# Attention beside a gated linear unit on one core: the score tiles of a period in another order, the first one whole, two of them under one exponential

## The chip, the core and the metric

The kernel runs on one core of a Trainium2 chip. The metric is the device time of one execution in microseconds (us); for the kernel before it is 1671.07 us, the median of three runs (1670.6 to 1671.36). The core's engines work side by side, each through its own list of instructions: PE multiplies matrices (PEld is its loading of weights), ACT (ScalarE) evaluates functions such as the exponential, DVE (VectorE) reduces and combines, POOL (GpSimd) does elementwise work on the on-chip memory SBUF, SP issues DMAs. Matrix products land in PSUM, which has eight banks of 128 x 512 float32 each. Before an engine writes a bank again, those who read it must be done, and they tell so by semaphores.

## The reference

For `x` of 2048 tokens by 512 (float32):

```
q, k, v = split(x @ wqkv)                # 32 heads of width 16
p = softmax(q @ k.T / 4)                 # per head, 2048 x 2048
a = concat_heads(p @ v) @ wo
b = (sigmoid(x @ w_gate) * (x @ w_up)) @ w_down      # inner width 1792
g = sigmoid(sum(x * gate_w))
out = g * a + (1 - g) * b
```

## The kernel before, in words

Most matrix products take float32 operands that are split into a high and a low part and sum three products of them. The kernel has three stretches: a head (projections of q, k, v and the first work on the scores), 256 **periods** of attention, and a tail that multiplies by `w_down` and `wo`.

A period `k` stands for 4 key tiles of 128 keys and 512 queries, for both heads of a pair. The scores of one key tile and one head are one matmul of 64 rows by 512 columns, which fills one bank (word `t0` for head 0 of the pair, `t1` for head 1, function `st_part`, lines 630 to 644); ACT turns the bank into exponentials in SBUF (line 643). To keep the exponentials in range each query needs the maximum of its scores: for it the scores are computed a second time with queries on the partitions (words `m0`, `m1`, function `sm_step`, line 299, 48 rows by 512 columns) and DVE reduces each bank to one column (line 301). These run ahead of the exponentials by a pair of heads. The products of the gated linear unit are the filler: words `d0`, `d1` (lines 153 and 173, 64 rows by 512 columns, into the eighth bank, `dn`), twelve in a period; when a run of twelve is done, ACT copies `dn` out (line 574).

A matmul of 64 or 48 rows uses one half of the PE's rows. Words that end in 0 use the lower half, words that end in 1 the upper half, and the two halves work at the same time. An even period has `t0` (both of the period's key groups of head 0), an odd one `t1`; the filler of a period goes to the other half.

At the end of a period stand the **values** (function `values`, line 781): 32 recorded matmuls over all 128 rows that multiply the exponentials of period `k` by `v` into one bank. ACT copies that bank to SBUF (line 786, tile `part` or `sum`), and POOL adds it up (line 799).

The order inside a period is written out by hand in the strings `STEADY` (one for even, one for odd periods, lines 835 and 836) and followed by `emit`; all engines but SP keep the order of the program. Seven banks are handed out in a ring by `place`: each `t`, each `m` and the values take the next bank. In the strings of before, the first score tile of a period is cut in two pieces of 192 and 320 queries (`CUT`), and each piece takes a bank of its own. So a period takes 9 `t`, 8 `m` and one bank for the values, 18 in all, and the values get the bank that the 11th tile of the same period had. `STEADY` holds for 248 periods; the last eight follow other strings (`LAST`, lines 837 and 838), with no `m` and nothing cut, and their banks come from the same ring.

Of the kernel before, what the change touches and what calls it, by code (L numbers as in the profile page):

```python
# [2 lines left out]

# [9 lines left out]
F32 = mybir.dt.float32  # L13
F32R = mybir.dt.float32r
AF = mybir.ActivationFunctionType
# [4 lines left out]
PSUM = bass.MemoryType.PSUM  # L20
DRAM = bass.MemoryType.DRAM
SHARED = "both halves of the PE write one bank"
SYNC = mybir.DependencyInfo(mybir.DependencyClass.Sync, mybir.DependencyReason.DATA)

S, D, H, DH, F = 2048, 512, 32, 16, 1792
P = 128
# [8 lines left out]
KR = 64  # L35
# [6 lines left out]
EARLY = NPER - TAIL - 4  # L42
LOW, UP = 0, 1
AHEAD = 4
CUT = (192,)
MIX = ((((0, 0), "+", (1, 1)), ((0, 0), None, None)), (((0, 1), "-", (1, 1)), ((1, 0), "-", (0, 0))),
       (((0, 0), "+", (0, 1)), ((1, 0), "+", (1, 1))), (((1, 1), None, None), ((1, 1), None, None)))
BLOCKS = (((0, 0), (1, 0)), ((1, 1), (1, 1)), ((0, 0), (1, 1)), ((1, 0), (0, 1)), ((0, 0), (0, 0)), ((0, 1), (0, 1)))
# [2 lines left out]
@with_exitstack  # L51
def gated_mix(ctx, tc, x, xc, xmix, wqk, wv, wo, w_gu, w_down, gate_w, out):
    nc = tc.nc
    pe, act, dve, pool, sp = nc.tensor, nc.scalar, nc.vector, nc.gpsimd, nc.sync

    ctx.enter_context(tc.manual_schedule(engines=ORDERED))
    keep = ctx.enter_context(tc.tile_pool(name="keep", bufs=1))
    dram = ctx.enter_context(tc.tile_pool(name="dram", bufs=1, space=DRAM))
    ps = ctx.enter_context(tc.tile_pool(name="ps", bufs=1, space=PSUM))

    def turns(tiles):
        turn = iter(range(1 << 30))
        return lambda: tiles[next(turn) % len(tiles)]
# [1 line left out]
    def ring(pool, n, shape, name):  # L65
        return turns([pool.tile(shape, F32, name=f"{name}{i}") for i in range(n)])

    banks = [ps.tile([P, 512], F32, name=f"st{i}") for i in range(3)]
    bank = turns(banks)
    dn = ps.tile([P, 512], F32, name="dn")  # L70
    bankd = turns([dn])
    maxb = [ps.tile([P, 512], F32, name=f"sm{i}") for i in range(4)]
    bankm = turns(maxb)

    q_d = dram.tile([2, D, S], F32, name="q_d")
    k_d = dram.tile([2, D, S], F32, name="k_d")
# [19 lines left out]
    def mid(name, dt=F32):  # L96
        return keep.tile([P, 4, 512], dt, name=name, tag="mid", bufs=3)
# [44 lines left out]
    class Sum:  # L142


        def __init__(self, o, ab):
            self.o, self.n, self.last, self.token = o, 0, None, None
            self.ops = list(terms(ab))
            self.left = [list(self.ops), list(self.ops)]

        def half(self, g):  # L150
# [3 lines left out]
            if self.token:  # L154
                tc.add_manual_dep(mm.ins, self.token.ins.name, SYNC, reason=SHARED)
            self.last, self.token = mm, None
# [34 lines left out]
    def turn(*runs):  # L191

        token = pool.nop()
        tc.add_manual_dep(token.ins, runs[-1].last.ins.name, SYNC, reason=SHARED)
        for r in runs:
# [179 lines left out]
    def take(n, behind=None):  # L375
        while parts and n:
            load = parts.pop(0)()
            if behind:
                tc.add_manual_dep(load.ins, behind.ins.name, SYNC, reason="one at a time")
            n -= 1  # L380
# [111 lines left out]
    def filling():  # L492
# [45 lines left out]
        for cp in range(2):  # L538
            for fp in range(NF // 2):
# [28 lines left out]
                if cp == 0 and fp == NF // 2 - 1:  # L568
# [9 lines left out]
    first = [(j, i) for j in [*range(0, 12, 2), *range(1, 8, 2), *range(12, FIRST, 2), *range(9, FIRST, 2),  # L578
                              *range(FIRST, UPPER, 2)] for i in range(2)]
# [11 lines left out]
    for c in range(NC):  # L591
# [9 lines left out]
        for w, dst in ((w_q, q_d), (w_k, k_d)):  # L601
            o = bank()
# [21 lines left out]
    for t in range(2):  # L624
        o = bankv()
# [1 line left out]
        put_v(t, o, act)  # L627
    ptile = {}

    def st_part(k, b, first=()):  # L630

        p, r = divmod(k, 16)
        c, kt = divmod(4 * r, 16)
        qs, ks = QS[p % 2], KS[p % 2]
        r = 64 * b
        pt = ptile[k, b] = mid(f"p{k}_{b}")
        for a in range(4):
            ends = [0, *(first if a == 0 else ()), 512]
            for lo, hi in zip(ends, ends[1:]):
                o = bank()[:, :hi - lo]  # L640
                pe.matmul(o, ks[r:r + KR, (kt + a) * P:(kt + a + 1) * P], qs[r:r + KR, c * 512 + lo:c * 512 + hi],  # L641
                          start=True, stop=True)
                act.activation(pt[:, a, lo:hi], o, AF.Exp, scale=DH ** -0.5)  # L643
                yield

    closed = []
    ahead = st_part(0, 1)
    bank = bankm
# [27 lines left out]

    for _, turned in closed:
        turned()()
    seven = [maxb[0], maxb[1], banks[2], maxb[2], banks[1], maxb[3], banks[0]]
    chunks = [(c, f) for c in range(NC) for f in range(0, NF, 2)]  # L680

    def hidden_load(c, f):
# [138 lines left out]
    def emit(order, **parts):  # L821

        for word in order.split():
# [7 lines left out]
            else:  # L831
                if next(parts[word], place) is place:
                    place()

    STEADY = ("t0 m1 t0 d1 t0 d1 m0 d1 t0 m0 d1 d1 t0 d1 work t0 m0 d1 t0 d1 m0 d1 t0 d1 m0 d1 t0 d1 m1 m0",
              "t1 m0 t1 d0 t1 d0 m1 d0 t1 d0 m1 t1 d0 d0 work d0 t1 m1 t1 d0 d0 d0 m1 t1 d0 m1 t1 d0 m1 m0")
    LAST = ["t0 d1 t0 d1 t0 d1 t0 d1 d1 work t1 t1 t1 t1", "t0 d1 t0 d1 t0 d1 t0 d1 work t1 t1 t1 t1"] * 2 + [
        "t0 t0 t0 t0 work t1 d0 t1 d0 t1 d0 t1 d0 d0", "t0 t0 t0 t0 work t1 d0 t1 d0 t1 d0 t1 d0"] * 2

    group = {"m0": mx(0), "m1": mx(1), "d0": dense(LOW), "d1": dense(UP)}  # L840
    for a, engine in enumerate((act, dve)):
        put_v(NS - 2 + a, two[a].o, engine)
    bank = bankm = place
    stages = [[], []]
    ahead_h = []
    for k in range(NPER):
        n = 2 * k
        if 320 <= n < 448 and n % 16 == 0:
            logit_load((n - 320) // 8)
        if n % 32 == 0 and n // 32 + 1 < NPAIR:  # L850
            pair = load_pair(n // 32 + 1)
        if n % 32 <= 10:
            list(islice(pair, 2))
        if k >= NPER - TAIL:
            group["t0"], group["t1"] = st_part(k, 0), st_part(k + 1, 1) if k + 1 < NPER else iter(())
        elif k % 2 == 0:
            group["t0"] = chain(st_part(k, 0, CUT), st_part(k + 1, 0))
        else:
            group["t1"] = chain(st_part(k, 1, CUT), st_part(k + 1, 1))
        emit(STEADY[k % 2] if k < NPER - TAIL else LAST[k - NPER], **group)  # L860
        jobs = [turned() for turned in stages.pop(0)]
        stages.append([])
        while full:
            halves, turned = close_max()
            jobs.append(halves)
            stages[1].append(turned)
        if run is None:
            pass
        elif run.done():
            run = next(fill, None)  # L870
        elif k < NPER - TAIL or k == NPER - TAIL + 3:
            turn(run)
        if EARLY <= k < EARLY + 6:
            for _ in range(2 if k < EARLY + 3 else 1):
                weights_ahead()
        if n in (304, 308, 312, 316):
            ahead_h.append(hidden_ahead((n - 304) // 4))
            next(ahead_h[-1])
        if n in (308, 312, 316, 320):
            next(ahead_h[(n - 308) // 4])  # L880
        work(3 if isinstance(run, Sum) and k % 2 else 4)
        urgent.extend(jobs)
        if 320 <= n < 448:
            t = (n - 320) // 16 * 2
            if n % 16 == 2:
                logit_terms(t, 0)
                logit_terms(t, 1)
            elif n % 16 in (8, 10):
                logit_sum(t, (n % 16 - 8) // 2)
        if EARLY <= k < EARLY + 4:  # L890
            early_exp(*divmod(k - EARLY, 2))
        if k == NPER - 1:
            break
        values(k)
        if k == EARLY - 2:
            loaded.extend(hidden_load(*chunks[m]) for m in range(2))
        if NPER - TAIL <= k < NPER - TAIL + 4:
            early_hidden(*divmod(k - NPER + TAIL, 2))
        if n == NSTEP - 16:
            raws = [late_raw(*late[m][:2]) for m in range(2)]  # L900
        if n == NSTEP - 10:
            denominators(0)
# [41 lines left out]
    bankt = turns([dn] + maxb[2:] + maxb[:2])  # L944
# [29 lines left out]
    heads = {}  # L974
    for n, (c, f) in enumerate(chunks):
        if f == 0:
            down = [bankt() if 4 * c + t != AHEAD else None for t in range(4)] if c else seven[3:]
        if n == 4:
            g = g0[:, AHEAD:AHEAD + 1]
            dve.tensor_scalar(ahead, dn, g, None, op0=ALU.mult)  # L980
        if n in at:
            heads_out(at[n], heads.pop(at[n]))
        hl = ready[n]
        for t in range(4):
            if 4 * c + t == AHEAD:
                continue
            ops = list(terms([((hl[0][a][:, t * P:(t + 1) * P], hl[1][a][:, t * P:(t + 1) * P]), wd[f + a])
                              for a in range(2)]))
            for m, (a, b) in enumerate(ops):
                pe.matmul(down[t], a, b, start=(f == 0 and m == 0), stop=(f == NF - 2 and m == 5))  # L990
            if f == NF - 2:
                finish(4 * c + t, down[t], g0)
            if n == t == 0:
                last_values()
        if n + 5 < len(chunks):
            loaded.append(hidden_load(*chunks[n + 5]))
        if n == 9:
            denominators(1)
        if n + 3 < len(chunks):
            hidden(n + 3)  # L1000
        if n + 2 < len(chunks):
            hidden_split(n + 2)
        if n + 3 in at:
            u = at[n + 3]
            heads[u] = heads_split(u, *heads[u])
        if n + 5 in at:
            u = at[n + 5]
            heads[u] = heads_load(u)
        late_next()
# [44 lines left out]
```

## Time and profile before

| | |
|---|---|
| median of three runs | 1671.07 us |
| profiled execution, its own time | 1671.01 us |
| its span (first to last instruction) | 1669.2 us |
| granted PE clock | 1.00 |
| first values of the 256 periods | at 90.17 us of the span |
| values of the 248th period | at 1444.57 us |
| busy between 84.6 and 1444.6 us (1360.0) | PE 1359.15, DVE 1237.68, ACT 1206.48, POOL 977.93 |

The busy time of PE counts any matmul in flight, and the ends of matmuls are modelled, so it does not tell whether both halves of the rows were in use. The profile's rows of the timeline read: start in us, duration in us, engine, line, operation, written tile, read tiles, shapes, how many; brackets give the idle time before and what ended it.

### The profile page before, as it was taken

The page shows a single profiled execution, that of the slowest core. Times are in us where ns is not written, and L with a number is a line of the kernel's source. Part 1 is how long each engine was busy: PE and PEld are TensorE (multiplying, and loading weights), DVE is VectorE, ACT ScalarE, POOL GpSimd, SP SyncE. Part 2 cuts the span into 40 slices and gives each one's busy share as a digit, 9 for nine tenths or more (in the row PEclk, how much of TensorE's full clock was granted, in tenths as well). Part 3 has the DMA queues.
Part 4 walks back from the last instruction along what each step waited for, and adds up shares of the span by engine and source line. Part 5 has one row for each costly group of instructions (what it writes and reads, how often), then busy time and mean ns, then how long its engine had stood idle before and what let it go on. Part 6 is the DMA issues. An engine that isn't in the chain of part 4 may idle for free.

```text
span 1669.2 us, 44610 instructions
## 1 busy us (share of the span) xinstructions
PE 1663.4 (100%) x16842; PEld 1174.6 (70%) x16842; DVE 1427.2 (85%) x2456; ACT 1334.1 (80%) x2928; POOL 1052.3 (63%) x1238
## 2 busy tenths in 40 slices
PE   9999999999999999999999999999999999999999
PEld 7866666666666666666666666666666666678887
DVE  6989999999999999999999999999999999667643
ACT  4188888888888888888888999999999988974421
POOL 1146665368878888776675897777776767752110
PEclk9999999999999999999999999999999999999999
DMA  9624667464444444442347453424243425268850
GB/s 261 131 81 159 190 204 197 131 159 141 122 146 134 128 140 131 126 119 75 93 152 198 138 138 109 120 90 103 90 100 96 109 84 178 76 228 299 286 185 26
DMA packets 131559, 236.74 MB, mean 142 GB/s; under 512 B 19408, under 2 KB 39888, under 8 KB 128336
## 3 DMA queue, kind: packets, MB, share of 16 engines
q1 hardware_dynamic: 131056, 233.37, 47.1%
q8 instruction: 133, 2.18, 0.6%
q14 instruction: 82, 0.67, 0.2%
q10 hardware_dynamic: 288, 0.52, 0.1%
HBM read 155.71 MB, written 77.59 MB: 140 GB/s over the span
## 4 chain that ended last, share of the span: by engine, by line
PE 99%; DVE 0%; ACT 0%; issue 0%; POOL 0%; ACTq 0%; DVEq 0%
PE dn L173 27%; PE sm L781 17%; PE st L781 13%; PE dn L153 7%; PE sm L299 6%; PE sm L641 6%; PE sm L990 6%; PE st L299 4%; PE st L641 4%; PE st L140 4%; PE dn L990 2%; PE st L153 2%; PE st L990 1%; PE st L88 0%; ACT p L643 0%; DVE stat L301 0%
## 5 line engine op out<-in xcount | busy, mean ns | idle before, releaser
L301 DVE TENSOR_REDUCE stat<-sm 128x1 f32<-128x512 f32 x1199 | 763.1, 681 | 77.2 <-PE st L641 49.8
L643 ACT ACTIVATE p<-sm 128x512 f32<-128x512 f32 (+1 forms) x1314 | 667.5, 595 | 5.5 <-PE sm L641 5.3
L301 DVE TENSOR_REDUCE stat<-st 128x1 f32<-128x512 f32 x849 | 549.2, 681 | 51.8 <-PE sm L641 51.4
L643 ACT ACTIVATE p<-st 128x512 f32<-128x512 f32 (+2 forms) x982 | 515.6, 596 | 1.0 <-PE st L641 0.5
L173 PE MATMUL dn<-xm,mh 64*128 64x512 f32 x1568 | 485.7, 389 | 0.0
L299 PE MATMUL sm<-ks,qs 48*128 48x512 f32 x1199 | 483.8, 427 | 0.1
L641 PE MATMUL sm<-qs,ks 64*128 64x512 f32 (+1 forms) x1314 | 471.6, 382 | 0.0
L299 PE MATMUL st<-ks,qs 48*128 48x512 f32 x849 | 363.5, 428 | 0.0
L641 PE MATMUL st<-qs,ks 64*128 64x512 f32 (+2 forms) x982 | 362.7, 382 | 0.6 <-DVE v L622 0.6
L173 PE MATMUL dn<-xm,ml 64*128 64x512 f32 x784 | 304.7, 389 | 0.0
L173 PEld LDWEIGHTS dn<-xm,mh 64*128 64x128 f32 x1568 | 290.0, 185 | 15.9
L781 PE MATMUL sm<-p,v 128*17 128x256 f32 x4672 | 280.6, 381 | 0.1
L641 PEld LDWEIGHTS sm<-qs,ks 64*128 64x128 f32 x1314 | 234.2, 187 | 63.9 <-DVE stat L301 58.8
L299 PEld LDWEIGHTS sm<-ks,qs 48*128 48x128 f32 x1199 | 210.8, 185 | 41.1 <-ACT p L643 34.5
L781 PEld LDWEIGHTS sm<-p,v 128*17 128x17 f32 x4672 | 123.1, 97 | 130.0 <-ACT p L643 44.6
L641 PEld LDWEIGHTS st<-qs,ks 64*128 64x128 f32 x982 | 177.8, 187 | 49.1 <-DVE stat L301 44.9
L781 PE MATMUL st<-p,v 128*17 128x256 f32 x3520 | 211.4, 381 | 0.1
L799 POOL TENSOR_TENSOR sum<-sum,part 128x256 f32<-128x256 f32 x192 | 141.5, 737 | 73.6 <-ACT part L786 45.6
L424 POOL TENSOR_TENSOR m<-m,m 128x512 f32<-128x512 f32 x140 | 178.3, 1291 | 5.0 <-ACT m L574 2.9
L299 PEld LDWEIGHTS st<-ks,qs 48*128 48x128 f32 x849 | 156.7, 185 | 28.3 <-ACT p L643 25.6
L781 PEld LDWEIGHTS st<-p,v 128*17 128x17 f32 x3520 | 92.8, 97 | 98.1 <-ACT p L643 33.5
L173 PEld LDWEIGHTS dn<-xm,ml 64*128 64x128 f32 x784 | 144.4, 184 | 10.3
(314 smaller groups left out, 2341.6 us busy)
## 6 DMA issues: line engine op xcount, KB each, us to landing
r<-in_w_gu_dram SPq DMA_DIRECT2D x112, 256.0 KB
gul<-gu_d SPq DMA_DIRECT2D x56, 512.0 KB
gu_d<-m SPq DMA_DIRECT2D x84, 256.0 KB
xm_d<-xm SPq DMA_DIRECT2D x32, 512.0 KB
xm<-xm_d SPq DMA_DIRECT2D x32, 512.0 KB
xm<-in_xmix_dram SPq DMA_DIRECT2D x24, 512.0 KB
qs<-q_d SPq DMA_DIRECT2D x90, 128.0 KB
ks<-k_d SPq DMA_DIRECT2D x90, 128.0 KB
```

The lines of the kernel that those rows point to most:

```text
L140: pe.matmul(o, a, b, start=(i == 0), stop=(i == len(ops) - 1))
L153: mm = pe.matmul(self.o, a[rows], b[rows], start=(self.n == 0), stop=(self.n == 2 * len(self.ops) - 1))
L173: pe.matmul(self.o, a, b, start=(self.n == 0), stop=(self.n == len(self.ops) - 1))
L299: pe.matmul(t, qs[r:r + KM, qt * P:(qt + 1) * P], ks[r:r + KM, g * 512:(g + 1) * 512], start=True, stop=True)
L301: dve.tensor_reduce(stat[part][:, qt % 4, g:g + 1], t, axis=AX.X, op=ALU.max)
L424: pool.tensor_tensor(o, x, y, op)
L641: pe.matmul(o, ks[r:r + KR, (kt + a) * P:(kt + a + 1) * P], qs[r:r + KR, c * 512 + lo:c * 512 + hi], start=True, stop=True)
L643: act.activation(pt[:, a, lo:hi], o, AF.Exp, scale=DH ** -0.5)
L781: pe.matmul(o[r:r + VW, :], v[:, 4 * k % 16 + a, h * VW:(h + 1) * VW], pts[b][:, a, 256 * i:256 * i + 256], start=(a == 0), stop=(a == 3))
L799: pool.tensor_tensor(s, s, e, ALU.add)
L990: pe.matmul(down[t], a, b, start=(f == 0 and m == 0), stop=(f == NF - 2 and m == 5))
```

## The change

The kernel after makes four edits.

1. All seven banks of the ring are one PSUM tile `st` of 7 x 512 columns. A small class `Apart` stands around PE, ACT and DVE: it declares that two instructions of different engines on different banks of this tile don't depend on each other, and adds the dependency where PE and another engine touch the same bank.
2. The first score tile is no longer cut. A period takes 8 `t`, 8 `m` and the values: 17 banks. The values get the bank that the 10th tile of the period had.
3. The third and fourth key tile of a period's first group (`JOINT = 2`) lie in neighbouring banks and share one exponential over 128 x 1024, except where the third lies in the ring's last bank; then each has its own.
4. The strings `STEADY` are new. In even periods five `m0` and three `m1` stand where six and two stood, in odd periods five `m1` and three `m0`.

The tail's first four accumulators become banks 0 to 3 of the ring in place of 3 to 6. By 17 tiles in place of 18 over 248 periods the ring stands three banks further back there, so each accumulator follows the same work as before.

```diff
-CUT = (192,)
+JOINT = 2
-    banks = [ps.tile([P, 512], F32, name=f"st{i}") for i in range(3)]
-    maxb = [ps.tile([P, 512], F32, name=f"sm{i}") for i in range(4)]
+    st = ps.tile([P, 7, 512], F32, name="st")
+    seven = [st[:, i, :] for i in range(7)]
+    touched = deque(maxlen=64)
+    latest = [{} for _ in seven]
+    class Apart:
...
+            def call(*args, **kw):
+                ins = op(*args, **kw)
+                rows, tiles = set(), set()
...
+                if rows:
+                    for engine, others, theirs, other in touched:
+                        if engine is not self.engine and not rows & others and not tiles & theirs:
+                            tc.declare_no_dep(ins.ins, other.ins, reason=OTHER)
+                    for row in rows:
+                        for engine, other in latest[row].items():
+                            if engine is not self.engine and nc.tensor in (engine, self.engine):
+                                tc.add_manual_dep(ins.ins, other.ins.name, SYNC, reason=SAME)
+                        latest[row][self.engine] = ins
+                    touched.append((self.engine, rows, tiles, ins))
+                return ins
...
-    def st_part(k, b, first=()):
+    def st_part(k, b, joint=None):
...
-            ends = [0, *(first if a == 0 else ()), 512]
-            for lo, hi in zip(ends, ends[1:]):
-                o = bank()[:, :hi - lo]
-                pe.matmul(o, ks[r:r + KR, (kt + a) * P:(kt + a + 1) * P], qs[r:r + KR, c * 512 + lo:c * 512 + hi],
-                          start=True, stop=True)
-                act.activation(pt[:, a, lo:hi], o, AF.Exp, scale=DH ** -0.5)
-                yield
+            o = bank()
+            scores(o, a)
+            if a == joint and o is not seven[-1]:
+                first = place_of(o)
+            elif first is not None:
+                assert o is seven[first + 1]
+                act.activation(pt[:, a - 1:a + 1, :], st[:, first:first + 2, :], AF.Exp, scale=DH ** -0.5)
+                first = None
+            else:
+                act.activation(pt[:, a, :], o, AF.Exp, scale=DH ** -0.5)
+            yield
...
-    STEADY = ("t0 m1 t0 d1 t0 d1 m0 d1 t0 m0 d1 d1 t0 d1 work t0 m0 d1 t0 d1 m0 d1 t0 d1 m0 d1 t0 d1 m1 m0",
-              "t1 m0 t1 d0 t1 d0 m1 d0 t1 d0 m1 t1 d0 d0 work d0 t1 m1 t1 d0 d0 d0 m1 t1 d0 m1 t1 d0 m1 m0")
+    STEADY = ("m1 t0 t0 d1 m0 d1 d1 t0 d1 t0 m0 d1 t0 d1 m0 work d1 d1 t0 d1 d1 t0 d1 m0 d1 t0 m1 m1 m0",
+              "t1 m0 m0 t1 d0 m1 d0 t1 t1 d0 d0 d0 t1 d0 m1 work d0 t1 t1 d0 d0 m1 d0 m1 d0 m1 d0 t1 m0")
...
-            down = [bankt() if 4 * c + t != AHEAD else None for t in range(4)] if c else seven[3:]
+            down = [bankt() if 4 * c + t != AHEAD else None for t in range(4)] if c else seven[:4]
```

More of the change, by code (lines that the diff above doesn't have):

```diff
@@ L1 @@
+from collections import deque
 from contextlib import ExitStack
@@ L22 @@
 SHARED = "both halves of the PE write one bank"
+OTHER = "another bank of the same tile"
+SAME = "the same bank"
 SYNC = mybir.DependencyInfo(mybir.DependencyClass.Sync, mybir.DependencyReason.DATA)
@@ L53, in gated_mix @@
     nc = tc.nc
-    pe, act, dve, pool, sp = nc.tensor, nc.scalar, nc.vector, nc.gpsimd, nc.sync
+    pool, sp = nc.gpsimd, nc.sync
     ctx.enter_context(tc.manual_schedule(engines=ORDERED))
     keep = ctx.enter_context(tc.tile_pool(name="keep", bufs=1))
+    ps = ctx.enter_context(tc.tile_pool(name="ps", bufs=1, space=PSUM))
     dram = ctx.enter_context(tc.tile_pool(name="dram", bufs=1, space=DRAM))
-    ps = ctx.enter_context(tc.tile_pool(name="ps", bufs=1, space=PSUM))
     def turns(tiles):
@@ L66, in ring, with __init__, __getattr__, place_of @@
         return turns([pool.tile(shape, F32, name=f"{name}{i}") for i in range(n)])
-    banks = [ps.tile([P, 512], F32, name=f"st{i}") for i in range(3)]
-    bank = turns(banks)
+    st = ps.tile([P, 7, 512], F32, name="st")
     dn = ps.tile([P, 512], F32, name="dn")
     bankd = turns([dn])
-    maxb = [ps.tile([P, 512], F32, name=f"sm{i}") for i in range(4)]
+    seven = [st[:, i, :] for i in range(7)]
+    touched = deque(maxlen=64)
+    latest = [{} for _ in seven]
+    class Apart:
+        def __init__(self, engine):
+            self.engine = engine
+        def __getattr__(self, name):
+            op = getattr(self.engine, name)
+            def call(*args, **kw):
+                ins = op(*args, **kw)
+                rows, tiles = set(), set()
+                for a in chain(args, kw.values()):
+                    if isinstance(a, bass.AP) and a.tensor is st.tensor:
+                        first = a.offset % (7 * 512) // 512
+                        rows.update(range(first, first + (2 if a.ap[1] == (512, 2) else 1)))
+                    elif isinstance(a, bass.AP):
+                        tiles.add(a.tensor.name)
+                if rows:
[9 more added lines that the diff above has]
+                return ins
+            return call
+    pe, act, dve = [Apart(engine) for engine in (nc.tensor, nc.scalar, nc.vector)]
+    banks = [seven[i] for i in (6, 4, 2)]
+    bank = turns(banks)
+    maxb = [seven[i] for i in (0, 1, 3, 5)]
     bankm = turns(maxb)
+    def place_of(o):
+        return next(i for i, other in enumerate(seven) if other is o)
     q_d = dram.tile([2, D, S], F32, name="q_d")
@@ L636, in st_part, with scores @@
         pt = ptile[k, b] = mid(f"p{k}_{b}")
+        def scores(o, a):
+            pe.matmul(o, ks[r:r + KR, (kt + a) * P:(kt + a + 1) * P], qs[r:r + KR, c * 512:(c + 1) * 512],
+                      start=True, stop=True)
+        first = None
         for a in range(4):
-            ends = [0, *(first if a == 0 else ()), 512]
-            for lo, hi in zip(ends, ends[1:]):
-                o = bank()[:, :hi - lo]
-                pe.matmul(o, ks[r:r + KR, (kt + a) * P:(kt + a + 1) * P], qs[r:r + KR, c * 512 + lo:c * 512 + hi],
-                          start=True, stop=True)
-                act.activation(pt[:, a, lo:hi], o, AF.Exp, scale=DH ** -0.5)
-                yield
+            o = bank()
[5 more added lines that the diff above has]
+                act.activation(pt[:, a - 1:a + 1, :], st[:, first:first + 2, :], AF.Exp, scale=DH ** -0.5)
+                first = None
+            else:
+                act.activation(pt[:, a, :], o, AF.Exp, scale=DH ** -0.5)
+            yield
     closed = []
@@ L678, in gated_mix @@
         turned()()
-    seven = [maxb[0], maxb[1], banks[2], maxb[2], banks[1], maxb[3], banks[0]]
     chunks = [(c, f) for c in range(NC) for f in range(0, NF, 2)]
@@ L856, in gated_mix @@
         elif k % 2 == 0:
-            group["t0"] = chain(st_part(k, 0, CUT), st_part(k + 1, 0))
+            group["t0"] = chain(st_part(k, 0, JOINT), st_part(k + 1, 0))
         else:
-            group["t1"] = chain(st_part(k, 1, CUT), st_part(k + 1, 1))
+            group["t1"] = chain(st_part(k, 1, JOINT), st_part(k + 1, 1))
         emit(STEADY[k % 2] if k < NPER - TAIL else LAST[k - NPER], **group)
```

## The prediction

> **What bounds the kernel now.** I read the page first: PE is in flight for the whole span, and the chain of work that ended last runs almost wholly along it.
>
> ```profile
> span 1669.2 us, 44610 instructions
> PE 1663.4 (100%) x16842; PEld 1174.6 (70%) x16842; DVE 1427.2 (85%) x2456; ACT 1334.1 (80%) x2928; POOL 1052.3 (63%) x1238
> PE 99%; DVE 0%; ACT 0%; issue 0%; POOL 0%; ACTq 0%; DVEq 0%
> ```
>
> That doesn't mean that PE sets the time: a busy PE may have one half of its rows idle, and its weight loads may wait. So I read the timeline of one period (an odd one, from values to values), then the loads that waited, and last a period of `LAST`, which does without `m` and without the cut. Between the first and the 248th values, in front of PE, lie 247 periods:
>
> ```profile
> 90.17 0.41 PE L781 MATMUL sm<-p,v 128*17 128x256 f32 x4
> ...
> 1444.57 1.92 PE L781 MATMUL st<-p,v 128*17 128x256 f32 x32
> ```
>
> (1444.57 - 90.17) / 247 = 5.483 us for a period. All times below count from the start of a period's values, which here is 803.13. ACT in that period:
>
> ```profile
> 805.18 0.38 ACT L786 ACTIVATE part<-sm 128x256 f32<-128x256 f32 x1 [0.63 <-PE sm L781]
> 805.46 0.33 ACT L643 ACTIVATE p<-st 128x192 f32<-128x192 f32 x1
> 805.67 0.45 ACT L643 ACTIVATE p<-sm 128x320 f32<-128x320 f32 x1
> 805.99 0.62 ACT L643 ACTIVATE p<-st 128x512 f32<-128x512 f32 x1
> 806.46 0.64 ACT L643 ACTIVATE p<-st 128x512 f32<-128x512 f32 x1
> 806.94 0.65 ACT L643 ACTIVATE p<-st 128x512 f32<-128x512 f32 x1
> 807.41 0.66 ACT L643 ACTIVATE p<-sm 128x512 f32<-128x512 f32 x1
> 807.89 0.67 ACT L643 ACTIVATE p<-st 128x512 f32<-128x512 f32 x1
> ```
>
> PE in the same period:
>
> ```profile
> 803.13 1.43 PEld L781 LDWEIGHTS sm<-p,v 128*17 128x17 f32 x32 [0.30 <-ACT p L643]
> 804.98 0.18 PEld L641 LDWEIGHTS st<-qs,ks 64*128 64x128 f32 x1 [0.42 <-DVE stat L301]
> 804.99 0.50 PE L299 MATMUL sm<-ks,qs 48*128 48x512 f32 x1
> 805.32 0.39 PE L173 MATMUL dn<-xm,mh 64*128 64x512 f32 x1
> ...
> 806.47 0.39 PE L173 MATMUL dn<-xm,ml 64*128 64x512 f32 x1
> 806.51 0.39 PE L641 MATMUL sm<-qs,ks 64*128 64x512 f32 x1
> 806.70 0.39 PE L173 MATMUL dn<-xm,mh 64*128 64x512 f32 x1
> ...
> 807.84 0.39 PE L173 MATMUL dn<-xm,ml 64*128 64x512 f32 x1
> ...
> 808.13 0.50 PE L299 MATMUL sm<-ks,qs 48*128 48x512 f32 x2
> 808.62 0.41 PE L781 MATMUL st<-p,v 128*17 128x256 f32 x4
> ```
>
> The values start at 808.62, 0.05 after the exponential of 807.89 has ended (807.89 + 0.67 = 808.56). That exponential belongs to the 11th tile of the period, and the values stand in tile 18: seven banks on, so the same bank. This is **the bound**: values, copy of their bank (+2.05), then seven exponentials in a row, the seventh from +4.76 to +5.43, bank free, values again at +5.48. That is the 5.483. PE alone would have been sooner: its half with the filler carries 14 matmuls (12 `d`, two `m`), and the waits named in the brackets, on ACT, took the rest.
>
> DVE is close behind but has room: its eight reductions are followed by idle time.
>
> ```profile
> 805.52 4.87 DVE L301 TENSOR_REDUCE stat<-sm 128x1 f32<-128x512 f32 x8 [0.62 <-PE sm L641]
> ...
> L301 DVE TENSOR_REDUCE stat<-sm 128x1 f32<-128x512 f32 x1199 | 763.1, 681 | 77.2 <-PE st L641 49.8
> ```
>
> **PE's own end of a period.** What PE needs when no bank is late shows in `LAST`:
>
> ```profile
> 1446.61 0.38 ACT L786 ACTIVATE part<-st 128x256 f32<-128x256 f32 x1 [0.61 <-PE st L781]
> 1447.02 0.60 ACT L643 ACTIVATE p<-sm 128x512 f32<-128x512 f32 x1
> 1447.51 0.60 ACT L643 ACTIVATE p<-st 128x512 f32<-128x512 f32 x1
> ```
>
> ```profile
> 1446.42 0.50 PE L641 MATMUL sm<-qs,ks 64*128 64x512 f32 x1
> 1446.76 0.40 PE L641 MATMUL st<-qs,ks 64*128 64x512 f32 x1
> ...
> 1448.16 0.40 PE L641 MATMUL st<-qs,ks 64*128 64x512 f32 x1
> 1448.40 0.39 PE L641 MATMUL sm<-qs,ks 64*128 64x512 f32 x1
> 1448.71 0.41 PE L781 MATMUL st<-p,v 128*17 128x256 f32 x4
> ```
>
> From the last matmul of a half to the values it is 1448.71 - 1448.40 = 0.31. From the values to the second matmul of each half it is 2.19 (804.99 is the first `m`, 805.32 the first `d` in that half; 805.32 - 803.13 = 2.19; 1446.76 - 1444.57 = 2.19). Twelve `d` in a row take 807.84 - 805.32 = 2.52 from first to last (0.229 each). One `t` after another takes 1448.40 - 1448.16 = 0.24, so 0.23 to 0.24.
>
> **The change part by part.**
>
> *The order* is what costs. Counting the strings by their last digit: before, the fuller halves of an even period held 12 `d1` and 2 `m1`, beside 8 whole `t0` and 6 `m0`: 14 each. After, an even period has 12 `d1` + 3 `m1` = 15 in the upper half and 8 `t0` + 5 `m0` = 13 in the lower; an odd one 15 (`d0`, `m0`) in the lower and 13 in the upper. The work is the same over two periods, but the values need all rows and close each period, so the halves can't even out across them. PE's own end becomes:
> - even: first `m1`, then `d1` from 2.19 to 2.19 + 2.52 = 4.71, then two `m1` at 4.94 and 5.18 (0.23 to 0.24 each), values at 5.18 + 0.31 = 5.49;
> - odd: two `m0`, the second at 2.19, `d0` from 2.43 to 4.95, the last `m0` at 5.18, values at 5.50.
>
> Before it would have been 2.19 + 2.52 + 0.23 + 0.31 = 5.25: the 0.24 of one more matmul eats all the room that PE had under ACT's 5.48. Bounds: by the spacing between 806.47 and 806.70, 0.23 or a little less throughout, the even period ends at 5.45; by 0.234, the spacing of `t` in `LAST` ((1448.40 - 1446.76) / 7), throughout, 13 steps give 2.19 + 3.04 + 0.31 = 5.54. I take the row of twelve `d`, since that is what stands there.
>
> *The first tile whole.* It saves a fixed cost on ACT (0.21 and 0.32 for the pieces, 0.48 for a whole one), but the first exponential starts later: a piece of 192 was there when the copy of the values was through (+2.33); a whole tile starts at 1447.02 - 1444.57 = 2.45.
>
> *The shared exponential.* No row shows one over two banks. From start to start the rows have 0.21 for 192 columns, 0.32 for 320 and 0.477 for 512 ((807.89 - 805.99) / 4), so 0.00083 a column and some 0.05 fixed: 0.477 + 0.427 = 0.90 for 1024, against 0.95 for two. Lower bound 0.90; upper bound 1.05, the time of a lone 1024-wide function from start to end:
>
> ```profile
> L739 ACT ACTIVATE gul<-gul 128x1024 f32<-128x1024 f32 x26 | 27.2, 1048 | 2.4 <-DMA gul<-gu_d 2.4
> ```
>
> I take 0.90, because all of ACT's rows here overlap and fit one line. The values now follow the 10th tile, in both strings the sixth `t`: exponentials at 2.45, 2.94 (1447.51 - 1447.02 = 0.49), the pair at 3.42, then 4.32, and the 10th tile at 4.80; with 0.64 to its end (fifth in a row, as at 806.46) and 0.05 to the load, values at 5.48 to 5.49. So ACT's end stands where it stood: 0.12 later at the start, 0.10 less work behind it (0.05 from the cut, 0.05 from the pair), and the rest is rounding. Nothing comes free there. At an upper price of 1.05 it would be 5.63.
>
> *One time in seven* the third tile falls in the last bank and the pair is not made: 0.05 to 0.06 more, ACT's end at 5.54.
>
> *The banks of the other words.* The pair gives both banks back at its end, 3.42 + 0.90 + 0.14 = 4.46 (0.14 is what a tile's 0.62 at 805.99 lasts beyond the 0.48 to the next). Tile 12 of the even period and tiles 13 and 14 of the odd one wait for that; they stand in the half of 13, or at 4.7 and later, and none of them reaches the values. Should it come 0.1 later, nothing changes. The sequencer holds what stands behind a waiting load, the `d` of the other half among it; at tile 12 that `d` is due at 4.71, so 0.2 of room. DVE's eight reductions stay, their first at +2.39 as now (805.52 - 803.13), 0.6 idle.
>
> *One PSUM tile and `Apart`* add no instruction. If all false dependencies are declared away, they cost nothing; a dependency that is left would show as a new wait (a rival below). The ring's shift in the tail goes with the tail's accumulators: nothing. POOL and SP's DMAs are not moved past anything; the copies, adds and `work` keep their number.
>
> **Sum.** Six periods in seven at (5.49 + 5.50) / 2 = 5.495, one at 5.54: 5.502. Against 5.483: +0.019 x 247 = +4.7 us. Head, `LAST` and tail as before. From the profiled 1671.01 us (the median of the runs shown is 1671.07, the span 1669.2, so 1.8 lies around it) that is 1675.7; I say 1676.
>
> **A rule against the rows.** In this period the `d` at 806.70 stands ahead of the `t` at 806.51 in the program (the seventh `d0` of the string before, and the `t1` behind it), and starts after it: the halves go each by its own list. The Trainium skill says otherwise: "TensorE: Matmul & The Clock Gate", section "The mechanism", has matmuls start and end strictly in program order. This case's trace disagrees (806.51 before 806.70). By that rule the sum would be that of the fifth rival, 1681.
>
> **The rivals.**
>
> 1. *No change.* PE's fuller half runs a little tighter than now, since the other half has only 13, and ACT's end, unmoved at 5.48, stays the bound: for it, the 0.23 between 806.47 and 806.70, where the halves are out of step; against, the mean of the twelve, 0.229, and that pairs aren't always made. 1670 to 1674.
> 2. *Faster.* The same tightening to 0.226, which puts PE at 2.19 + 13 x 0.226 + 0.31 = 5.44, decides once ACT's end falls under it as well: the whole first tile would have to start 0.06 sooner, at the 0.03 to 0.04 that DVE's reduction takes after its matmul (804.99 + 0.50 = 805.49, reduction at 805.52), not the 0.10 that the first exponential took. Then 5.455 a period, -0.025 x 247 = -6: 1665. Against: 2.45 is a row.
> 3. *The pair saves nothing or costs.* ACT's end at 5.53 (two times 0.477) to 5.63 (1.05): +0.05 to +0.15 a period, 1684 at the lower end, 1708 at the upper. For: no row shows a read over two banks. Against: the straight line through 192, 320 and 512.
> 4. *The change doesn't do what it says:* dependencies left over in the one tile make PE wait for exponentials or reductions of other banks. At one extra wait of 0.3 a period (the bracket of the values' load) that would be +74, 1745. Against: the list of 64 covers more than a period's accesses, and an older access has long ended.
> 5. *A late bank in one half holds the other.* In the odd period tile 10 (`t1`) takes the bank of tile 3, which the second reduction frees at 2.39 + 0.61 + 0.68 = 3.68 (0.61 is 4.87 / 8); it is due at 2.19 + 7 x 0.229 = 3.79, with 0.18 for its load ahead, so some 0.05 late. Were the halves bound to one order, the `d0` behind it would lose as much, 0.025 a period on the mean, +6: 1681. Against: 806.51 and 806.70 above.
>
> **How the numbers follow.** Forecast (PE's end, 1673.5 to 1681) 0.42; no change 0.29; faster 0.16; pair without gain 0.09; left-over waits 0.02; one order 0.02. The range from 1664 to 1688 takes in the bounds of the matmul spacing (5.45 and 5.54) and of the pair at its nearer end. Within 0.2% (3.3 us), about what a measurement of this kernel can tell from no change, lies the rival of no change and a small part of the forecast: 0.31; faster 0.16; slower 0.53.
>
> **What would show it.** Right: values to values at 5.49 to 5.51 in the common period; the load of the values waiting for no exponential, or by less than 0.05; the fuller half without gaps; ACT idle 0.6 as before, the pair's row at about 1.03 long and 0.90 to the next. Wrong: values that still start 0.05 after the 10th tile's exponential with PE's halves done before; a gap of the fuller half at tile 12 or 14; new releasers in the loads' brackets; a period under 5.47.

## The result and the profile after

The kernel after takes 1684.26 us (median, 1683.74 to 1684.68) where the one before takes 1670.82 (1670.16 to 1671.36): 1.008 times as long, 95% interval 1.0068 to 1.0091, or 13.4 us slower. The forecast of 1676 had the sign and, of the loss, little more than a third.

Of the kernel after, the head of the page, and the shares that lines have in the chain of work that ended last:

```profile
span 1682.3 us, 43221 instructions
PE 1676.0 (100%) x16594; PEld 1156.4 (69%) x16594; DVE 1451.0 (86%) x2456; ACT 1326.1 (79%) x2467; POOL 1052.0 (63%) x1238
PE st L87 72%; PE dn L87 26%; ACT p L87 0%; DVE stat L87 0%; DVE acc L87 0%; DVE v L87 0%; DVE mt L87 0%; ACT v L87 0%; POOL mxs L146 0%; POOL mxs L145 0%; DVE mxs L87 0%; DVE warm L87 0%; ACTq L87 0%
```

All of PE, ACT and DVE now stand on line 87, that of the class's `call`, so groups are told apart by tile and shape. ACT works 8 us less than before, and yet the span is 13 us longer. The groups of exponentials show that the pairs are made, 213 in 248 periods, six in seven:

```profile
L87 ACT ACTIVATE p<-st 128x512 f32<-128x512 f32 x1622 | 849.2, 622 | 16.9 <-PE st L87 9.3 <-PE dn L87 1.1
L87 ACT ACTIVATE p<-st 128x1024 f32<-128x1024 f32 x213 | 219.9, 1032 | 0.1
```

Where the time went shows in PE's rows of the first, the 248th and the last values. After, then before (the row of the last values; the other two stand in the prediction):

```profile
90.78 0.41 PE L87 MATMUL st<-p,v 128*17 128x256 f32 x4
...
1454.16 0.41 PE L87 MATMUL st<-p,v 128*17 128x256 f32 x4
...
1491.40 0.41 PE L87 MATMUL st<-p,v 128*17 128x256 f32 x4
```

```profile
1478.26 0.63 PE L781 MATMUL st<-p,v 128*17 128x256 f32 x8
```

| stretch | before | after | more |
|---|---|---|---|
| start to the first values | 90.17 | 90.78 | 0.6 |
| 247 periods | 1354.40 (5.483 each) | 1363.38 (5.520 each) | 9.0 |
| 248th to last values | 33.69 | 37.24 | 3.5 |
| last values to the end | 190.9 | 190.9 | 0.0 |

So two places: 0.036 in each period, and 3.5 us in the last eight, which the forecast had left as they were. The 0.6 of the head can't be put down to the change: in the traces of all the kernels below the first values come between 89.98 and 90.96, and at 90.64 in one that differs from the kernel before only in what follows the first values. From here on a time in a period counts from the start of its values. The medians of even and odd periods, worked out from the starts of all values, are 5.53 and 5.50 after (5.49 and 5.47 before).

An even period after (values at 803.37), ACT's timeline; the row of 128x1024 is the pair:

```profile
805.42 0.38 ACT L87 ACTIVATE part<-st 128x256 f32<-128x256 f32 x1 [0.70 <-PE st L87]
805.85 0.60 ACT L87 ACTIVATE p<-st 128x512 f32<-128x512 f32 x1
806.34 0.59 ACT L87 ACTIVATE p<-st 128x512 f32<-128x512 f32 x1
806.82 1.03 ACT L87 ACTIVATE p<-st 128x1024 f32<-128x1024 f32 x1
807.72 0.62 ACT L87 ACTIVATE p<-st 128x512 f32<-128x512 f32 x1
808.20 0.63 ACT L87 ACTIVATE p<-st 128x512 f32<-128x512 f32 x1
```

and PE's in the same period, its first matmuls and its end:

```profile
805.22 0.50 PE L87 MATMUL st<-ks,qs 48*128 48x512 f32 x1
805.22 0.50 PE L87 MATMUL st<-qs,ks 64*128 64x512 f32 x1
805.56 0.39 PE L87 MATMUL dn<-xm,mh 64*128 64x512 f32 x1
...
808.10 0.39 PE L87 MATMUL dn<-xm,ml 64*128 64x512 f32 x1
...
808.33 0.40 PE L87 MATMUL st<-ks,qs 48*128 48x512 f32 x1
...
808.57 0.39 PE L87 MATMUL st<-ks,qs 48*128 48x512 f32 x1
808.89 0.41 PE L87 MATMUL st<-p,v 128*17 128x256 f32 x4
```

This is the forecast's own walk, a little longer: first `d` at +2.19, twelve `d` in 2.54, two `m` 0.23 and 0.24 apart, values 0.32 behind the last. ACT's exponential of tile 10 ends at 808.83, 0.06 before the values, so the two ends are a few hundredths apart. The pair takes 0.90 to the next exponential, as the straight line through the narrower ones had it.

An odd period after (values at 797.88), PE's weight loads, then DVE's third reduction, then two of ACT's exponentials, the first of the period and that of tile 10:

```profile
801.64 0.18 PEld L87 LDWEIGHTS st<-qs,ks 64*128 64x128 f32 x1
...
802.24 0.18 PEld L87 LDWEIGHTS st<-ks,qs 48*128 48x128 f32 x1 [0.15 <-DVE stat L87]
...
802.57 0.18 PEld L87 LDWEIGHTS st<-ks,qs 48*128 48x128 f32 x1
...
803.37 0.13 PEld L87 LDWEIGHTS st<-p,v 128*17 128x17 f32 x7 [0.35 <-ACT p L87]
```

```profile
801.50 0.68 DVE L87 TENSOR_REDUCE stat<-st 128x1 f32<-128x512 f32 x1
```

```profile
800.26 0.60 ACT L87 ACTIVATE p<-st 128x512 f32<-128x512 f32 x1
...
802.62 0.63 ACT L87 ACTIVATE p<-st 128x512 f32<-128x512 f32 x1
```

The load at 802.24 is that of tile 12: it starts 0.06 after the reduction of its bank has ended (802.18), and four matmuls of that half, its own the first of them, are still to come. The values' bracket names ACT, but tile 10's exponential had ended 0.12 before (802.62 + 0.63 = 803.25): here the bracket names the last semaphore, not what held PE.

### The profile page after: what moved, and what is told of

It is laid out like the page before. It is cut to its first block, busy times and chain, and to the rows that moved or that the text cites. A ratio compares the mean times of both kernels' runs of the same rounds, so it can differ in the third digit from the quotient of the medians.

```text
span 1682.3 us, 43221 instructions
## 1 busy us (share of the span) xinstructions
PE 1676.0 (100%) x16594; PEld 1156.4 (69%) x16594; DVE 1451.0 (86%) x2456; ACT 1326.1 (79%) x2467; POOL 1052.0 (63%) x1238
## 4 chain that ended last, share of the span: by engine, by line
PE 99%; DVE 0%; ACT 0%; issue 0%; POOL 0%; ACTq 0%
PE st L87 72%; PE dn L87 26%; ACT p L87 0%; DVE stat L87 0%; DVE acc L87 0%; DVE v L87 0%; DVE mt L87 0%; ACT v L87 0%; POOL mxs L146 0%; POOL mxs L145 0%; DVE mxs L87 0%; DVE warm L87 0%; ACTq L87 0%
## 5 line engine op out<-in xcount | busy, mean ns | idle before, releaser
L87 DVE TENSOR_REDUCE stat<-st 128x1 f32<-128x512 f32 x2048 | 1270.6, 683 | 116.3 <-PE st L87 113.2
L87 ACT ACTIVATE p<-st 128x512 f32<-128x512 f32 (+1 forms) x1835 | 1017.6, 670 | 17.0 <-PE st L87 9.3
L87 PE MATMUL st<-qs,ks 64*128 64x512 f32 x2048 | 700.3, 414 | 1.2 <-DVE v L87 1.2
L87 PE MATMUL st<-ks,qs 48*128 48x512 f32 x2048 | 670.7, 419 | 0.1
L87 PE MATMUL st<-p,v 128*17 128x256 f32 x8192 | 495.4, 381 | 0.2
L87 PEld LDWEIGHTS st<-qs,ks 64*128 64x128 f32 x2048 | 349.4, 185 | 83.4 <-ACT m L87 41.1
L87 PEld LDWEIGHTS st<-ks,qs 48*128 48x128 f32 x2048 | 332.3, 184 | 106.6 <-issue 44.0
L87 PEld LDWEIGHTS st<-p,v 128*17 128x17 f32 x8192 | 216.6, 97 | 238.1 <-ACT p L87 87.9
L168 POOL TENSOR_TENSOR ml<-r,mh 128x512 fp32r<-128x512 f32 x112 | 144.0, 1285 | 7.0
L87 ACT ACTIVATE m<-dn 128x512 f32<-128x512 f32 x196 | 130.9, 668 | 0.0
```

The costliest lines, as they stand in the source:

```text
L87: ins = op(*args, **kw)
L168: pool.tensor_tensor(l, src, h.bitcast(F32), ALU.subtract)
```

## The experiments

Behind each time stands its ratio to that of the kernel before on the same chip, with the 95% interval. The theory behind the forecast (P) had PE's half of 15 matmuls as what sets a period; the rivals were ACT with its later first tile and its pair (A), and waits left over from the one PSUM tile (D).

**The one tile alone.** The kernel before, with the tile `st` and the class:

```diff
-    banks = [ps.tile([P, 512], F32, name=f"st{i}") for i in range(3)]
-    maxb = [ps.tile([P, 512], F32, name=f"sm{i}") for i in range(4)]
+    st = ps.tile([P, 7, 512], F32, name="st")
...
+    pe, act, dve = [Apart(engine) for engine in (nc.tensor, nc.scalar, nc.vector)]
```

> The kernel before, with its strings, its cut and its 18 banks a period, but with the seven banks as one PSUM tile and the class around the engines. Theory P (in the attention periods PE's half of 15 matmuls sets the time; the one tile costs only in the last eight periods, where the values wait for a whole set of exponentials at once): periods as before at 5.48, the last eight +3.5 us, so 1674 to 1675. Rival A (ACT's first tile and pair set the periods, and the last eight are late for the same reason): 1671, as before. Rival D (the one tile leaves waits everywhere): 1680 to 1685.

Measured: 1675.01 us, 1.0025 (1.0016 to 1.0034). Periods 5.483, as before; the last eight 37.3 us. So the tile costs nothing in the 247 periods and all of the 3.5 us behind them.

**Why the last eight.** There a period's values come soon after their own exponentials. In the kernel after, PE's loads of the first such values, and those of before:

```profile
1458.26 0.12 PEld L87 LDWEIGHTS st<-p,v 128*17 128x17 f32 x4 [0.35 <-ACT p L87]
1458.66 1.41 PEld L87 LDWEIGHTS st<-p,v 128*17 128x17 f32 x28 [0.28 <-ACT p L87]
1460.50 0.18 PEld L87 LDWEIGHTS st<-qs,ks 64*128 64x128 f32 x1 [0.42 <-issue]
```

```profile
1448.71 1.43 PEld L781 LDWEIGHTS st<-p,v 128*17 128x17 f32 x32 [0.36 <-ACT p L643]
1450.56 0.18 PEld L641 LDWEIGHTS sm<-qs,ks 64*128 64x128 f32 x1 [0.42 <-issue]
```

Before, the 32 loads run through, and the next tile's load comes 1.85 after the first. After, they stop behind the fourth for 0.28 on ACT, and the next tile's comes after 2.24. The first four belong to the other head, whose exponentials were made a period earlier. The fifth load is the first that reads this period's own exponentials; it starts 0.05 after the last of its head's four has ended (1457.99 + 0.62 = 1458.61):

```profile
1457.99 0.62 ACT L87 ACTIVATE p<-st 128x512 f32<-128x512 f32 x1
```

The class declares two instructions free of each other only if they share no other tile; a value matmul and an exponential share the tile `p` that holds four key tiles, so the matmul for the first key tile is left to wait for the exponential of the fourth. The remedy tells the four apart:

```diff
+    scored = set()
...
-                        tiles.add(a.tensor.name)
+                        parts = range(1)
+                        if a.tensor.name in scored:
+                            part = a.offset % 2048 // 512
+                            parts = range(part, part + (2 if a.ap[1:] == ((512, 2), (1, 512)) or a.shape[1:] in ((2, 512), [2, 512]) else 1))
+                        tiles.update((a.tensor.name, n) for n in parts)
...
+        scored.add(pt.tensor.name)
```

> The kernel after, but the class tells the four key tiles within one tile of exponentials apart, so that a value matmul is declared free of the exponentials that it does not read. Theory P: the last eight periods back from 37.2 to 33.7 us between the 248th and the 256th values, the rest unchanged: 1680 to 1681. Rival A (the last eight are late for another reason): 1684. Rival D (left-over waits cost in every period): 1675 or less.

Measured: 1680.91 us, 1.006 (1.0044 to 1.0077); the last eight 33.65 us, periods 5.521. The 3.5 us are explained by that, and the 9 us of the periods are not touched.

**The order alone.** The kernel before with one word of each string changed:

```diff
-    "... t0 d1 m0 d1 t0 d1 m1 m0"      "... d0 m1 t1 d0 m1 t1 d0 m1 m0"
+    "... t0 d1 m1 d1 t0 d1 m1 m0"      "... d0 m1 t1 d0 m0 t1 d0 m1 m0"
```

> The kernel before with one word of each string changed: the even string's last m0 but one becomes m1, the odd string's last m1 but one becomes m0, so that the filler's half has 15 matmuls and the other 13, as in the kernel after; banks, cut and exponentials stay. Theory P: PE's own end moves from 5.25 to some 5.52, past ACT's 5.48: +0.03 to +0.04 in each of 247 periods, 1678 to 1681. Rivals A and D: the order does not matter, 1671 to 1672.

Measured: 1678.25 us, 1.0042 (1.0027 to 1.0057); periods 5.510. With nothing changed on ACT, DVE or the banks, the fifteenth matmul of a half makes the old kernel 7.3 us slower, 6.6 of them in the 247 periods. It moves PE's end from below ACT's to above it. The last matmul of the fuller half and the values, then ACT's exponential of the tile whose bank they take, in one period:

```profile
807.12 0.39 PE L299 MATMUL sm<-ks,qs 48*128 48x512 f32 x1
807.44 0.41 PE L781 MATMUL sm<-p,v 128*17 128x256 f32 x4
```

```profile
806.71 0.67 ACT L643 ACTIVATE p<-sm 128x512 f32<-128x512 f32 x1
```

The values start 0.32 behind PE's last matmul, about as closely as in `LAST` (0.31), and 0.07 or 0.08 behind that exponential (medians of even and odd periods). In the kernel before it was the other way round: 0.45 or 0.47 behind PE's last matmul, and 0.05 behind the exponential.

**The pair alone.** The kernel after with `JOINT = None`:

> The kernel after without the shared exponential: two of 512 columns in its place, order and banks unchanged. Theory Q with the pair worth 0.05: ACT's end in even periods 5.51 to 5.56 and past PE's 5.53, odd ones unchanged at 5.50: +0.02 a period on the mean, 1686 to 1689. Rival (the pair saves nothing): 1684. Rival (the pair costs more than two): under 1683.

Measured: 1690.97 us, 1.012 (1.0104 to 1.0136), 2 us past the upper end. Even periods are 5.58 (5.53 with the pair), odd 5.51 or 5.52 (5.50). The pair does save what it should, and the rest of the change would be 20 us slower without it.

**One filler less.** The kernel after, with 14 matmuls in the fuller half:

```diff
...
+            if self.n == 5:
+                self.n += 1
+                return
             pe.matmul(self.o, a, b, start=(self.n == 0), stop=(self.n == len(self.ops) - 1))
...
```

> The kernel after without the sixth of every twelve filler matmuls in the attention periods (so the gated products lack one term of their sums): 14 matmuls in the fuller half in place of 15, nothing else moved. Theory P: the odd periods fall from 5.50 to ACT's end at 5.42 to 5.45, the even ones from 5.53 to 5.51: 1684 falls to between 1670 and 1676. Rivals A and D: PE is not what they wait for, 1683 to 1684.

Measured: 1681.25 us, 1.0062 (1.0047 to 1.0077). A miss: only 3 us of the 8 to 14 came back; even periods 5.51, odd 5.49. So P was not the whole of it: when PE's 15 go, something else stands almost as high. In this run, the weight loads of tile 12 and of the values in an odd period; then, in an even one, the exponential of tile 10 and the load of the values:

```profile
811.65 0.18 PEld L87 LDWEIGHTS st<-ks,qs 48*128 48x128 f32 x1 [0.30 <-DVE stat L87]
...
812.79 0.13 PEld L87 LDWEIGHTS st<-p,v 128*17 128x17 f32 x8 [0.32 <-ACT p L87]
```

```profile
806.61 0.63 ACT L87 ACTIVATE p<-st 128x512 f32<-128x512 f32 x1
```

```profile
807.29 0.13 PEld L87 LDWEIGHTS st<-p,v 128*17 128x17 f32 x8 [0.30 <-ACT p L87]
```

In the odd period tile 12 waits 0.30 for DVE, and the values follow 1.14 after it, as they did after (803.37 - 802.24 = 1.13). In the even one the values start 0.05 after tile 10's exponential has ended (806.61 + 0.63 = 807.24). That gave the theory Q of the next three runs: PE's 15 matmuls, DVE's third reduction in odd periods, ACT's tenth tile in even ones, each ending within a few hundredths of the others.

**The three limits one by one.** DVE lighter with one filler less, DVE lighter with all fillers, ACT lighter with one filler less:

```diff
-            dve.tensor_reduce(stat[part][:, qt % 4, g:g + 1], t, axis=AX.X, op=ALU.max)
+            dve.tensor_reduce(stat[part][:, qt % 4, g:g + 1], t[:, :256] if steady else t, axis=AX.X, op=ALU.max)
...
```

```diff
-                act.activation(pt[:, a, :], o, AF.Exp, scale=DH ** -0.5)
+                cols = slice(0, 256 if steady and joint is None and a == 0 else 512)
+                act.activation(pt[:, a, cols], o[:, cols], AF.Exp, scale=DH ** -0.5)
...
```

> The run without the sixth filler (1681.25 us, even periods 5.51, odd 5.49), and in the attention periods DVE reduces 256 of the 512 columns of each bank (half of the scores are left out of the maxima). Theory Q (the periods after have limits that nearly tie: PE's 15 matmuls; in odd periods also DVE's third reduction, which frees the bank of tile 12 with four matmuls still to come in that half; in even periods also ACT's exponential of tile 10, whose bank the values take): the odd periods fall from 5.49 to 5.41 to 5.48, the even ones stay at 5.51, 1671 to 1678. Rival P (the 15 matmuls alone, the rest is something else): no change, 1680 to 1682.

Measured: 1673.63 us, 1.0017 (1.0007 to 1.0026); odd periods 5.42, even ones 5.51 or 5.52, as Q had it. In one of its odd periods, the exponential of tile 10 and the values:

```profile
802.14 0.63 ACT L87 ACTIVATE p<-st 128x512 f32<-128x512 f32 x1
```

```profile
802.82 0.41 PE L87 MATMUL st<-p,v 128*17 128x256 f32 x4
```

The values start 0.05 behind that exponential (802.14 + 0.63 = 802.77), so here ACT is what is left. Odd periods without a pair are at 5.48, since ACT's work is longer in them.

> The kernel after with all its filler, and DVE reducing 256 of 512 columns in the attention periods (half of the scores left out of the maxima). Theory Q: with 15 matmuls in the fuller half PE alone holds the periods where they are, 5.53 even and 5.50 odd: 1683 to 1684.5. A rival in which DVE sets the periods by itself: 1675 or less.

Measured: 1681.27 us, 1.0063 (1.0045 to 1.0081), 2 us under the expected range; even periods 5.51, odd 5.49. So PE's 15 hold the odd periods when DVE is out of the way, against 5.42 with one filler less. The even periods also fell, by some 0.015: the twelve fillers of an even period took 2.52 in place of 2.55 on the median, and the values start 0.05 behind tile 10's exponential, so that ACT holds them. Why the fillers are closer when DVE reads less stays open.

> The run without the sixth filler (1681.25 us), and the exponential of a period's fifth score tile (tile 8) taken over 256 of 512 columns (the values use the first half twice in place of the rest), which takes 0.21 us from ACT ahead of tile 10. Theory Q: the even periods fall from 5.51 to between 5.42 and 5.46 (then tile 12 behind the pair's end is next), the odd ones stay at 5.49 on DVE: 1669 to 1675. Rival (ACT does not hold the even periods): no change, 1680 to 1682.

Measured: 1669.71 us, 0.9993 (0.9983 to 1.0002); even periods 5.44, odd 5.49. As Q had it again: even periods are ACT's once PE is out of the way.

| periods (median, us) | even | odd |
|---|---|---|
| after | 5.53 | 5.50 |
| one filler less | 5.51 | 5.49 |
| DVE lighter | 5.51 | 5.49 |
| one filler less, DVE lighter | 5.515 | 5.42 |
| one filler less, ACT lighter | 5.44 | 5.49 |

In each kind of period two ends lie almost together, PE's and ACT's in even ones, PE's and DVE's in odd ones. Taking PE's or DVE's away alone gives back 3 us of the 13 (ACT's alone was not taken away); taking away both of a kind brings that kind down, to 5.44 or 5.42. The distance from the end of tile 10's exponential to the values says the same for the kernel after itself: 0.05 where ACT holds PE, but 0.06 in its even periods with a pair and 0.13 to 0.14 in its odd ones, on the median.

**The old kernel's bound.** The kernel before with one filler less:

> The kernel before without the sixth of every twelve filler matmuls in the attention periods (the gated products lack one term of their sums). If ACT's chain from the copy of the values to the exponential of tile 11 alone sets the periods before, as the prediction reads them, nothing changes: 1670 to 1671.5, periods 5.48. A rival in which PE's 14 matmuls bind it: 1660 or less.

Measured: 1671.15 us, 1.0001 (0.9992 to 1.001); periods 5.483. So before, PE's 14 are not what sets the period, as the prediction read it.

**A faster one.** If ACT's chain from the copy of the values sets the old periods, then the copy itself can leave it:

```diff
         def copy(e):
-            if k < NPER - TAIL:
-                act.activation(e, o, AF.Copy)
-            else:
-                dve.tensor_copy(e, o)
+            dve.tensor_copy(e, o)
```

> The kernel before with the copy of the values on DVE in all periods in place of ACT. ACT's chain then begins when the first piece of 192 is there (2.21 + 0.10 = 2.31) and not when its copy is through (2.33): 0.02 a period less, 1664 to 1668. Against it: DVE gets 0.34 more work beside eight reductions of 0.60, and its first reduction comes 0.1 to 0.3 later; if tile 12's bank or a later one then waits, 1680 or more.

Measured: 1666.59 us, 0.9974 (0.9964 to 0.9984): faster than both kernels, by 4.3 and 17.7 us. On the median even and odd periods are both 5.46; in the kernel before they are 5.49 and 5.47.

> As the run with the copy on DVE, and the first score tile cut at 96 in place of 192 columns: the first piece is there sooner (some 2.13), so ACT's chain may begin at 2.23 and the second piece, 416 wide, ends at 2.79 in place of 2.86: 0.06 to 0.07 a period less than before, 1654 to 1660. If the second piece is late on PE or DVE's delay counts: 1665 or more.

Measured: 1669.1 us, 0.999 (0.9981 to 0.9999), a miss: the piece of 96 starts 0.05 sooner, but the second, 416 wide, waits for its own matmul, which ends at +2.41, so its exponential starts at +2.45, ACT's chain stays within 0.02 of where it was, and the periods are 5.475.

## Why the prediction was right or wrong

- *What bounds the kernel before*: right. One filler less changed nothing, and an earlier start of ACT's chain, by 0.02 on the mean, gave 0.018 a period on the mean (5.483 to 5.465).
- *The order is what costs*: right as a cause, shown by itself on the old kernel alone (7.3 us). In the sum, odd periods came at the 5.50 that the walk gave. Even ones came at 5.53 in place of 5.49: the term of the walk that was too small is the spacing in the fuller half, 2.54 for the twelve fillers and 0.47 for the two `m`, with 0.32 to the values, where 2.52, 0.47 and 0.31 were taken from rows of `LAST` and of a half with two `m`. Some 0.035 in 123 even periods is the larger half of the 8 us that the forecast was short. With the spacing as forecast ACT's end, 5.51 in these periods, would still have held them 0.02 above 5.49. The one period in seven without the pair, put at 5.54, came at 5.58 when even and at 5.50 when odd.
- *"Head, `LAST` and tail as before"*: wrong, by 3.5 us in the last eight periods. The fourth rival named the mechanism, a dependency left over in the one tile, but set it into the attention periods and dismissed it by the list's length; the leak is in the other condition of the class, the shared tile. The range, 1664 to 1688, held the time, but its upper end was set for the matmul spacing and the pair, not for this wait.
- *"None of them reaches the values"* (the banks of the other words): wrong. The walk had tile 10 of the odd period some 0.05 late on DVE, and left it there because that half has only 13 matmuls. But tile 12 behind it waits again, for the third reduction, and what is left of the half then ends with the other one. In the kernel as it is this costs nothing visible; it is why a filler less gave back 3 us and not 8 to 14.
- *"ACT's end stands where it stood"*, 5.48 to 5.49: true of neither kind of period. In even ones it is 5.51, since the first exponential starts at 805.85 - 803.37 = 2.48 and not at 2.45; in odd ones, where it starts at 800.26 - 797.88 = 2.38, it is 5.42.
- *The pair at 0.90*: right (807.72 - 806.82). By the Trainium skill, "ScalarE: Activation LUTs", section "What ACT_TABLE_LOAD costs", an ACTIVATE with immediate scale and bias takes 186 ns and 0.833 ns a column, and two in a row overlap by about 93 ns. By these figures a pair would save an estimated 93 ns; here it saves 0.05 of two times 0.48, so the trace has about half.
- *Faster* at 0.16: it needed a tighter spacing on PE, which came out wider in even periods (2.54 for the twelve), and a first exponential 0.06 sooner, which came in odd periods alone (2.38).

## What to carry to other kernels

When a change takes work off the engine that binds, work out the ends of the others to the same hundredth first: here two of them lay within some 0.02 us of each other in each kind of period, so that taking one of them away gave back little. A barrier that needs the whole array (here the values) makes the halves count one by one: work that balances over two periods does not balance within one. When several buffers become one tile, look for every pair of instructions that still shares some other tile, above all in stretches where the distance between writer and reader is short.

## What the runs showed of the hardware

An ACT instruction's start after PE's end went with how many semaphores it waits for, in these rows; no run changed that number alone. In the kernel after, the first score matmul of the even period ends at 805.72 (805.22 + 0.50) and its exponential, with two waits, starts 0.13 later; in the odd period, with one wait, it is 0.04. The copy of the values in the kernel before has the same step, 0.13 with two waits and 0.07 with one, and the periods that begin with the shorter one are 5.46 long, the others 5.49.
